# Second weight tile of the first product: its words fetched in steps 13 to 16 and its conversion begun one step later

## The chip, the cores and the metric

The kernel runs on one core of a Trainium2 chip. The metric is the device time of one execution in microseconds (us); smaller is better. The engines are named as in the profile: PE is the matrix engine (PEld its weight loads), DVE the vector engine, ACT the scalar engine, POOL the GpSimd engine, SP the engine that issues nearly all DMAs.

## The reference

Two blocks in a row. First a linear attention over 4 batches, 8 heads, 768 positions and 64 channels, worked through in blocks of 64 positions with a running state; then a mixer on the attention's output, seen as 4 x 768 x 512.

```
intra = einsum(q_b, k_b) * decay mask;  intra = einsum(intra, v_b)
inter = einsum(q_b * lam_pow, kv_state);  x = intra + inter
kv_state = lam_block * kv_state + einsum(k_b * rev_pow, v_b)
...
h = x^T @ U @ V                     (rank 32, along the 768 positions)
u = x + h^T
out = u + max(u @ w_ch1, 0) @ w_ch2 (512 -> 2048 -> 512)
```

q, k, v and lam are 32-bit floats. U, V, w_ch1 and w_ch2 arrive as 64-bit floats[...], so the kernel turns the 64-bit words into 32-bit floats itself.

## The kernel before, in words

**Stages.** The front stage (up to about 119 us of the span) does the attention and the mixer's low-rank part in 24 steps, one for each 128 positions of a batch: step s belongs to batch s // 6 and to position c = s % 6 in it. Then comes the first product u @ w_ch1 (`hidden`, L718), whose 16 weight tiles of 128 columns (`ft` = 0 to 15) meet six groups of 512 rows; its results go to HBM. Then the second product (`product`, L856) reads them back.

**One weight tile.** `w1_steps` (L232) gives the steps that make tile `ft` ready: four fetches of its 64-bit words (`fetch_part`, L129, one DMA of 128 KB each on SP), then the conversion on DVE: `one` (L153: L160), `mantissa` (L147: L149), `two` (L178), `three` (L186), `four` (L191), and the split of the 32-bit value into a high, a low and a combined part: `five` (L209), `six` (L217), `seven` (L224). Two of these hand something to ACT through `on_scalar` (L81): `one` hands over two activations that work out the exponent (L167, L168), `five` hands over a copy of the high part (L212). `three` reads what L168 wrote.

**How ACT's part is put off.** `aside(s)` (L650) runs the steps listed for step s; while it does, `on_scalar` only notes ACT's work. `on_scalar_late` (L656), in the list as `("late", s)`, then issues what was noted. From step 7 on there is one `late` in every step; it stands after `turned` and before the `aside` of the same step. So ACT's part of what `aside` does in step s is issued in step s + 1.

**One step of the front stage.** The order of all engines' work up to the first units of the first product is written out by hand (`pieces`, L561 to L583, under `manual_schedule`, L662). For s from 13 on it is: `prep(s+1)`: PE turns q and k (L355) into the PSUM banks "pq" and "pk", ACT copies them out (L358, `qt` then `kt`), and SP issues the next q and k loads; `scale(s+1)` on POOL (L383, L372); for c = 1 `fade(s)`, four activations on ACT (L392); `mix` (PE L514, DVE L517); for c = 0 `low` (PE L469, into bank "pq") and `low_rows` (DVE L489); `intra` (PE L453, then ACT's copy L458); `state` (PE L418 into bank "pk", DVE L424 or L426, SP's next v load); `turned` (ACT L550, POOL L551); `late`; `scores` (PE L400); `aside`; `inter` (PE L441); `masked` (DVE L409); `fade(s+1)` (ACT L392); `turn` (PE L531, SP's store of u L534, DVE L536 and L547). For c = 0 three pieces `next_of_low` come between (ACT L500 and L501, DVE L495, ACT L504); the result feeds the `mix` of the step after. Each of "pq" and "pk" is one bank that serves several uses in turn, so a use waits until the one before has been read out.

**Where the second tile stands.** The list at L640 to L645 says in which step each piece is run: for tile 1 the fetches in steps 8, 9, 10, 11, then `one` in 16, `mantissa` in 17, `two` in 19, `three` in 20, `four` in 21, `five` in 22, `six` in 23, and `seven` after step 23: it is `last` (L689) and runs after unit 0 of the first product (L801, L808). The first product's units 0 and 1 use tile 0, units 2 and 3 use tile 1.

Of the kernel before, what the change touches and what calls it, by code (L numbers as in the profile page):

```python
# [18 lines left out]
def kernel(  # L19
# [32 lines left out]
    NT = S // P  # L52
# [7 lines left out]
    NS = B * NT  # L60
# [18 lines left out]
    late = []  # L79
# [117 lines left out]
    def split_steps(tile_of, src, in_parts=False, scale=None, apart=False):  # L197

        st = {}

        def dst():
            if "w" not in st:
                st["w"] = wconv.tile([P, C], FP32, tag="wf", name="wf")
            return st["w"]

        def five():
            st["t"] = t = wconv.tile([P, C], FP32, tag="wt", name="wt")
            st["o"] = o = tile_of()
            nc.vector.tensor_scalar(  # L209
                t.bitcast(U32), st["w"].bitcast(U32), HI, None, ALU.bitwise_and  # L210
            )
            on_scalar(lambda: nc.scalar.copy(o[:, 0, :], t))  # L212

        def six():
            w, low = st["w"], st["o"][:, 1, :]
            st["low"] = low.bitcast(FP32) if scale is None else w
            nc.vector.tensor_tensor(  # L217
                out=low if scale is None else w, in0=w, in1=st["t"], op=ALU.subtract
            )
            if scale is not None:  # L220
                on_scalar(lambda: nc.scalar.mul(low, w, scale))

        def seven():
            nc.vector.scalar_tensor_tensor(  # L224
                st["o"][:, 2, :], st["t"], -E, st["low"], ALU.mult, ALU.add
            )

        return weight_steps(dst, src, C, in_parts=in_parts, apart=apart) + [five, six, seven]
# [3 lines left out]
    def w1_steps(ft, in_parts=False, apart=False):  # L232
        def tile_of():
            w1v[ft] = w1_pool.tile([P, 3, C], F32R, tag="w1", name="w1")
            return w1v[ft]

        cols = moe_w_ch1[:, ft * P : (ft + 1) * P].rearrange("(c p) f -> p c f", p=P)
        return split_steps(tile_of, cols, in_parts, apart=apart)
# [280 lines left out]
    uhl, ud, turned = {}, {}, {}  # L519
# [42 lines left out]
    for s in range(NS):  # L562
        b, c = divmod(s, NT)
        done = s - NT - 1
        more = s + 1 < NS
        step = [("prep", s + 1), ("scale", s + 1)] * more + [("fade", s)] * (c == 1)
        step += [("late", s - 1)] * (s == NT)
        step += [("mix", done)] * (0 <= done < NS - NT - 1)
        step += [("low", b - 1)] * (c == 0 and b > 0)
        step += [("low_rows", b - 1)] * (c == 0 and b > 0)  # L570
        step += [("intra", s)]
        step += [("next_of_low", b - 1)] * (c == 0 and b > 0)
        step += [("late", s)] * (s < NT - 1 or s == NT) + [("state", s)]
        step += [("next_of_low", b - 1)] * (c == 0 and b > 0)
        step += [("turned", done - 1)] * (done > 0) + [("late", s)] * (done >= 0)
        step += [("next_of_low", b - 1)] * (c == 0 and b > 0)
        step += [("scores", s + 1)] * more
        step += [("aside", s)] * (s >= 2 * NT)
        step += [("inter", s + 1), ("masked", s + 1)] * more
        step += [("fade", s + 1)] * (more and c > 0)  # L580
        step += [("aside", s)] * (s < 2 * NT)
        step += [("turn", done)] * (done >= 0 and done // TG < FG)
        pieces += step  # L583
# [13 lines left out]
    def v_steps():  # L597

        st = {}

        def dst():
            if "v" not in st:
                st["v"] = wconv.tile([P, C], FP32, tag="wf", name="vf")[0 : 2 * R, 0:SH]
            return st["v"]

        def parts(gs):
            for half in range(2):
                rows, cols = slice(half * R, (half + 1) * R), slice(half * SH, (half + 1) * SH)
                for g in gs:
                    yield v_hl[g * R : (g + 1) * R, cols], rows  # L610

        def five():
            st["t"] = t = wconv.tile([P, C], FP32, tag="wt", name="vt")[0 : 2 * R, 0:SH]
            nc.vector.tensor_scalar(
                t.bitcast(U32), st["v"].bitcast(U32), HI, None, ALU.bitwise_and
            )
            on_scalar(lambda: high(0))

        def high(g, copy=nc.scalar.copy):
            for out, rows in parts((g,)):  # L620
                copy(out, st["t"][rows])

        def low(g, engine):
            for out, rows in parts((g,)):
                engine.tensor_tensor(
                    out=out, in0=st["v"][rows], in1=st["t"][rows], op=ALU.subtract
                )

        halves = [moe_V[:, half * SH : (half + 1) * SH] for half in range(2)]
        return weight_steps(dst, halves, SH, 2 * R, in_parts=True) + [  # L630
            five, lambda: low(1, nc.vector), lambda: high(2, nc.vector.tensor_copy),
            lambda: low(3, nc.gpsimd),
        ]
# [5 lines left out]
    side = {}  # L639
    for steps, at in (  # L640
        (u_side, (-1, 1, 1, 2, 2)),
        (v_steps(), (0, 0, 3, 3, 4, 4, 4, 5, 4, 5)),
        (w1_steps(0, True), (3, 4, 5, 6, 8, 9, 10, 11, 13, 14, 15)),
        (w1_steps(1, True, True), (8, 9, 10, 11, 16, 17, 19, 20, 21, 22, 23, NS)),
    ):  # L645
        assert len(steps) == len(at)
        for step, n in zip(steps, at):
            side.setdefault(n, []).append(step)
# [7 lines left out]
    def on_scalar_late(s):  # L656
        for what in late:
            what()
        late.clear()
# [26 lines left out]
    run.update(aside=aside, late=on_scalar_late)  # L686
    for what, s in pieces:
        run[what](s)
    last = side.pop(NS)  # L689
    assert not side  # L690
    front_ctx.close()
# [106 lines left out]
        rest.append((unit, i, "turn", c0 + n))  # L798
    run["enter"] = enter_first_product
    head = [(pair, ft) for two in (pairs[:2], pairs[2:]) for ft in (0, 1) for pair in two]  # L800
    side = list(zip((0,), last)) + list(zip((0, 3, 3, 3, 4, 4, 4, 4), w1_steps(2)))  # L801
    for i, (pair, ft) in enumerate(head):
        before = {}
        for unit, n, *piece in rest:
# [14 lines left out]
    side = []  # L819
# [4 lines left out]
    side = w1_steps(FT - 1)  # L824
# [144 lines left out]
```

## Time and profile before

| | |
|---|---|
| median of 3 runs | 672.75 us (672.67 to 673.39) |
| the profiled execution, its own time | 673.08 us |
| its span | 671.3 us |
| PE busy | 665.1 us, 99% of the span |
| DVE, ACT, POOL busy | 74%, 41%, 17% |
| share of PE in the chain that ended last | 97% |
| steps 13 to 17: from one start of L453 to the next | 4.73 to 4.74 us |
| DMA in the stretch 40 to 104 us | mean 203 to 255 GB/s in stretches of 8 us |
| words of a weight tile, DMA of 128 KB, issue to landing | 3.0 to 4.8 us |

The timeline view gives one row for each run of like instructions: start, duration, engine, line, operation, tiles and count, and in brackets how long the engine stood idle before it and what released it. The matrix engine's rows overlap a little, since matmuls are pipelined: what matters is the start of one row against the start of the next. A wait is put down to the releaser that came last.

### The profile page before, as it was taken

To read this page: it belongs to the slowest core of one execution; us is meant where nothing else is said; L and a number is where in the kernel's file an instruction comes from. 1 tells how busy PE (TensorE), PEld (TensorE's weight loads), DVE (VectorE), ACT (ScalarE), POOL (GpSimd) and SP (SyncE) were. 2 spreads that over 40 slices of the span, in tenths; PEclk is the share of its full clock that TensorE was granted. 3 is DMA by queue.
4 is the path that set the end of the run, shared out by engine and by line. 5 is a ranking of instruction groups with operands and counts; after the bars stand their busy time and mean duration, and the time that the engine had idled before them with its cause. 6 is when DMAs were issued, how large, how long until landed. Compare 5 with 4: busy or idle time off the path is not lost.

```text
span 671.3 us, 13171 instructions
## 1 busy us (share of the span) xinstructions
PE 665.1 (99%) x5124; PEld 544.9 (81%) x5124; DVE 497.1 (74%) x873; ACT 277.3 (41%) x517; POOL 112.1 (17%) x92
## 2 busy tenths in 40 slices
PE   9999999999999999999999999999999999999997
PEld 7888989788888888888888888888888888888886
DVE  4689989877999777777797255786586775865864
ACT  4675767454555444444454121232222322322320
POOL 4465667340000000000000000030030300300300
PEclk9999999999999999999999999999999999999999
DMA  8999993254776555555577899854363363543431
GB/s 198 218 247 239 225 231 113 90 208 157 244 273 234 205 203 205 204 204 205 203 282 254 318 319 388 287 178 151 94 217 97 112 203 94 168 146 95 159 92 63
DMA packets 131775, 131.27 MB, mean 196 GB/s; under 512 B 81346, under 2 KB 89794, under 8 KB 131714
## 3 DMA queue, kind: packets, MB, share of 16 engines
q1 hardware_dynamic: 130512, 130.05, 61.2%
q8 instruction: 40, 0.66, 0.4%
q10 hardware_dynamic: 1202, 0.39, 0.2%
q14 instruction: 21, 0.17, 0.1%
HBM read 80.09 MB, written 50.33 MB: 194 GB/s over the span
## 4 chain that ended last, share of the span: by engine, by line
PE 97%; DVE 1%; DMA 1%; ACT 0%; issue 0%; ACTq 0%; DVEq 0%
PE pz L732 27%; PE pz L867 13%; PE pd L742 13%; PE pz L865 13%; PE pd L869 13%; PE px L453 4%; PE pss L400 4%; PE put L531 2%; PE pq L355 2%; PE px L441 2%; PE pk L355 1%; PE pkv L418 1%; PE pp L469 1%; PE pu L514 1%; DMA kraw<-in_k_dram 1%
## 5 line engine op out<-in xcount | busy, mean ns | idle before, releaser
L732 PE MATMUL pz<-u_hl,w 128*128 128x512 f32 x768 | 190.4, 397 | 0.0
L732 PEld LDWEIGHTS pz<-u_hl,w 128*128 128x128 f32 x768 | 144.0, 188 | 35.4 <-issue 0.4
L867 PE MATMUL pz<-w_hl,m 128*128 128x512 f32 x384 | 151.1, 396 | 0.0
L865 PE MATMUL pz<-w_hl,m 128*128 128x512 f32 x384 | 150.9, 396 | 0.0
L869 PE MATMUL pd<-w_d,m 128*128 128x512 f32 x384 | 149.5, 396 | 0.0
L848 ACT ACTIVATE m<-mt 128x512 fp32r<-128x512 f32 x96 | 60.5, 632 | 197.0 <-PE pd L869 148.9
L849 DVE SCALAR_TENSOR_TENSOR m<-rm,m 128x512 fp32r<-128x512 f32 x96 | 71.4, 746 | 53.7 <-ACT m L848 53.6
L894 POOL TENSOR_TENSOR o<-o,u 128x512 f32<-128x512 f32 x20 | 29.8, 1522 | 447.4 <-DVE o L890 447.4
L747 DVE SCALAR_TENSOR_TENSOR r<-pd,r 128x512 f32<-128x512 f32 x96 | 61.8, 686 | 53.2 <-ACT r L738 38.8
L742 PE MATMUL pd<-u_d,w 128*128 128x512 f32 x384 | 98.6, 397 | 0.0
L738 ACT ACTIVATE r<-pz 128x512 f32<-128x512 f32 x96 | 52.1, 596 | 92.7 <-PE pz L732 92.6
L867 PEld LDWEIGHTS pz<-w_hl,m 128*128 128x128 f32 x384 | 72.3, 188 | 17.7
L865 PEld LDWEIGHTS pz<-w_hl,m 128*128 128x128 f32 x384 | 72.3, 188 | 17.6
L869 PEld LDWEIGHTS pd<-w_d,m 128*128 128x128 f32 x384 | 72.3, 188 | 17.6
L742 PEld LDWEIGHTS pd<-u_d,w 128*128 128x128 f32 x384 | 72.1, 188 | 17.3
L850 DVE SCALAR_TENSOR_TENSOR m<-m 128x512 fp32r<-128x512 f32 x96 | 69.0, 721 | 0.9
L847 DVE TENSOR_SCALAR mt<-rm 128x512 uint32<-128x512 uint32 x96 | 46.1, 481 | 27.3 <-DMA rm<-r_d 26.9
L409 DVE TENSOR_TENSOR sm<-pss,mask 128x512 f32<-128x512 f32 x48 | 30.9, 685 | 7.9 <-PE pss L400 7.7
L212 ACT CAST w<-wt 128x512 fp32r<-128x512 f32 x32 | 19.9, 620 | 30.6 <-DVE wt L209 23.4
L383 POOL TENSOR_TENSOR qs<-qt,powq 128x512 f32<-128x512 f32 x20 | 26.0, 1298 | 22.0 <-ACT qt L358 19.0
L453 PEld LDWEIGHTS px<-vraw,sm 128*64 128x64 f32 x768 | 24.5, 138 | 5.2 <-issue 2.0
L400 PE MATMUL pss<-qt,kt 64*64 64x128 f32 (+1 forms) x576 | 28.1, 283 | 0.0
(88 smaller groups left out, 682.3 us busy)
## 6 DMA issues: line engine op xcount, KB each, us to landing
r_d<-r SPq DMA_DIRECT2D x96, 256.0 KB, 2.5
rm<-r_d SPq DMA_DIRECT2D x96, 256.0 KB, 2.7
words<-in_moe_w_ch_dram SPq DMA_DIRECT2D x30, 512.0 KB, 4.4
w_d<-w SPq DMA_DIRECT2D x16, 768.0 KB, 3.3
w_hl<-w_d SPq DMA_DIRECT2D x16, 512.0 KB, 6.6
vraw<-in_v_dram SPq DMA_DIRECT2D x24, 256.0 KB, 4.8
u_d<-x_nat SPq DMA_DIRECT2D x24, 256.0 KB, 3.6
u<-u_d SPq DMA_DIRECT2D x24, 256.0 KB, 3.8
```

The costliest lines, as they stand in the source:

```text
L400: nc.tensor.matmul(out=pss[rows, x, a, :], lhsT=kt[half[x], a, rows], rhs=qt[half[x], a, :], start=True, stop=True,)
L453: nc.tensor.matmul(out=px[half[t], x, a, :], lhsT=sm[:, x, a, half[t]], rhs=vr[:, 2 * a + x, :], start=(first and a == 0), stop=(a == HP - 1),
L732: nc.tensor.matmul(out=acc[g][0], lhsT=w[:, n, ct, :], rhs=uhl[g][:, n, ct, :], start=(ct == 0 and n == 0), stop=(ct == CT - 1 and n == 1),)
L738: nc.scalar.mul(rs[g], acc[g][0], 4096.0 + 1.0)
L742: nc.tensor.matmul(out=acc[g][1], lhsT=w[:, 2, ct, :], rhs=ud[g][:, ct, :], start=(ct == 0), stop=(ct == CT - 1),)
L747: nc.vector.scalar_tensor_tensor(rs[g], acc[g][1], 4096.0, rs[g], ALU.mult, ALU.add)
L848: nc.scalar.activation(out=m[:, 0], in_=t, func=AF.Relu)
L849: nc.vector.scalar_tensor_tensor(m[:, 1], r, 0.0, hi, ALU.max, ALU.subtract)
L850: nc.vector.scalar_tensor_tensor(m[:, 2], hi, E, low, ALU.mult, ALU.subtract)
L865: nc.tensor.matmul(out=pz, lhsT=m[:, 0, cols], rhs=hl[:, 0], start=first, stop=False)
L867: nc.tensor.matmul(out=pz, lhsT=m[:, 1, cols], rhs=hl[:, 1], start=False, stop=end)
L869: nc.tensor.matmul(out=pd, lhsT=m[:, 2, cols], rhs=dd, start=first, stop=end)
```

## The change

Eleven of the twelve places in the second tile's list change, and one `late` is left out. The four fetches go to steps 13 to 16, `one` to step 17, and all later pieces but `seven` one place on; `six` and `seven` both run after unit 0 of the first product. ACT's two activations (L167, L168), which `one` in step 17 hands over, would be issued by the `late` of step 18; that one is left out, so the `late` of step 19 issues them. `on_scalar_late(NS)` after the loop issues ACT's copy of the high part (L212), which `five` in step 23 hands over.

```diff
-        step += [("turned", done - 1)] * (done > 0) + [("late", s)] * (done >= 0)
+        step += [("turned", done - 1)] * (done > 0) + [("late", s)] * (done >= 0 and s != 3 * NT)
...
-        (w1_steps(1, True, True), (8, 9, 10, 11, 16, 17, 19, 20, 21, 22, 23, NS)),
+        (w1_steps(1, True, True), (13, 14, 15, 16, 17, 19, 20, 21, 22, 23, NS, NS)),
...
     for what, s in pieces:
         run[what](s)
+    on_scalar_late(NS)
     last = side.pop(NS)
...
-    side = list(zip((0,), last)) + list(zip((0, 3, 3, 3, 4, 4, 4, 4), w1_steps(2)))
+    side = list(zip((0, 0), last)) + list(zip((0, 3, 3, 3, 4, 4, 4, 4), w1_steps(2)))
```

| piece (line of its work) | step before | step after |
|---|---|---|
| four fetches (SP L140) | 8, 9, 10, 11 | 13, 14, 15, 16 |
| `one` (DVE L160) | 16 | 17 |
| ACT's L167, L168 | 17 | 19 |
| `mantissa` (DVE L149) | 17 | 19 |
| `two` (DVE L178) | 19 | 20 |
| `three` (DVE L186) | 20 | 21 |
| `four` (DVE L191) | 21 | 22 |
| `five` (DVE L209) | 22 | 23 |
| ACT's L212 | 23 | after step 23 |
| `six` (DVE L217) | 23 | after unit 0 |
| `seven` (DVE L224) | after unit 0 | after unit 0 |

No instruction is added or taken away, and the order of PE's and POOL's instructions stays as it was. Line numbers after L688 are one higher in the changed kernel, and after L801 still one higher.

## The prediction

> **What bounds the kernel now.** I read the page's engine shares and chain first, then the timelines of PE, ACT, DVE and SP around the moved pieces.
>
> ```profile
> PE 665.1 (99%) x5124; PEld 544.9 (81%) x5124; DVE 497.1 (74%) x873; ACT 277.3 (41%) x517; POOL 112.1 (17%) x92
> ...
> PE 97%; DVE 1%; DMA 1%; ACT 0%; issue 0%; ACTq 0%; DVEq 0%
> ```
>
> PE bounds every stage, so an edit that leaves PE's order alone changes the time only by the gaps it opens or closes in PE. In steps 13 to 17 the starts of L453 lie 4.73 to 4.74 us apart, every step: no gap there. The gaps of PE's timeline after 40 us are 0.16 us in step 12 (at 63.79) and 0.32 us in step 18:
>
> ```profile
> 93.35 0.60 PE L355 MATMUL pq<-ident,qraw 128*128 128x128 f32 x4
> ...
> 94.14 0.48 PE L514 MATMUL pu<-vp 128*128 128x512 f32 x1
> 94.94 1.52 PE L469 MATMUL pp<-x_nat,u_w 128*32 128x128 f32 x48 [0.32 <-ACT qt L358]
> ...
> 106.84 0.64 PE L418 MATMUL pkv<-vraw,ks 128*64 128x64 f32 x16
> ```
>
> The second row starts 0.80 us before the third, which needs bank "pq", and ACT empties it late. ACT's timeline says why, and shows the place where the same work goes:
>
> ```profile
> 92.95 0.71 ACT L167 ACTIVATE sc<-sc,vp 128x512 f32<-128x512 uint32 x1
> 93.70 0.72 ACT L168 ACTIVATE sc<-sc,vp 128x512 uint32<-128x512 f32 x1
> 94.33 0.56 ACT L358 COPY qt<-pq 128x512 f32<-128x512 f32 x1
> ...
> 103.69 1.05 ACT L392 ACTIVATE faded<-kv,powq 128x64 f32<-128x64 f32 x4
> 105.36 0.59 ACT L358 COPY qt<-pq 128x512 f32<-128x512 f32 x1 [0.62 <-PE pq L355]
> 105.84 0.59 ACT L358 COPY kt<-pk 128x512 f32<-128x512 f32 x1
> ```
>
> In step 17 the two activations stand right before the copy that frees "pq". In step 19 they will stand before the 103.69 row, where only 0.62 us of idle time is left until the next copies. The last two views are SP's and DVE's around the new place of the last fetch and of `one`:
>
> ```profile
> 87.66 0.97 SPq L279 DMA_DIRECT2D vraw<-in_v_dram  x1
> 88.73 1.71 SPq L534 DMA_DIRECT2D u_d<-x_nat  x1
> ```
>
> ```profile
> 91.85 0.42 DVE L149 TENSOR_SCALAR m<-words 128x512 uint32<-128x512 uint32 x1
> 92.99 1.29 DVE L409 TENSOR_TENSOR sm<-pss,mask 128x512 f32<-128x512 f32 x2 [0.73 <-PE pss L400]
> ...
> 96.60 1.23 DVE L489 TENSOR_SCALAR p_h<-pp 32x128 uint32<-32x128 uint32 x4 [0.40 <-PE pp L469]
> 98.06 0.42 DVE L424 COPY kv<-pkv 128x256 f32<-128x256 f32 x1 [0.23 <-PE pkv L418]
> ```
>
> The fetch of step 16 goes between the two SP rows; `one` takes the 91.85 slot. The brackets are the slack that DVE has behind it.
>
> **What the Trainium skill says.** "TensorE: Matmul & The Clock Gate", section on the array's architectural detail: ACT's and DVE's queues are strictly first in, first out. The trace agrees: qt's source was turned by 93.95, yet its copy started at 94.33, behind L168. "Perfetto Trace Analysis", section on HWDGE DMA instructions: an SP row is descriptor work after the waits, and the movement of the data is not in it; so arrival is taken from issue to landing (words: 3.0, 4.1, 4.8, 4.7, 3.4 us for the fetches of steps 6 and 8 to 11), never from the row. "SBUF — State Buffer", section on the two sides: a DVE operation with two SBUF inputs and a GpSimd one that reads SBUF shut each other out for a whole instruction. The trace agrees: L217 took 1.29 us beside POOL's L372 at 78.61, L224 1.52 us beside L544 at 131.01, against 0.68 us elsewhere.
>
> **Part 1, ACT's activations leave step 17: a gain.** In step 12, the same kind of step without them, L514 to L469 is 65.08 to 65.61, 0.53 us; in step 18 it is 0.80. Gain 0.80 - 0.53 = 0.27 us. Bounds: 0.20 (a part of the wait stays, since ACT still has copies to do), and 0.39 if L469 follows L514 as L453 does (41.16 to 41.57, 0.41 us). I take 0.27. Everything behind, ACT's chain too, moves forward with PE, so the offsets of later steps stay as they are.
>
> **Part 2, they enter step 19: a cost.** Tile 0 has the pair in the same place in step 9: L167 at 53.75, L392 at 55.12, so 1.37 us are put in. L392 goes from 103.69 to 105.06; L392 to qt is 0.95 us there (55.12 to 56.07), so qt starts at 106.01 instead of 105.36, 0.65 us late, and kt at 106.49, ending at 107.08. Queued behind: both copies, L458 and L550 of step 20. Who waits: PE's L418, which writes bank "pk" at 106.84 and needs kt's copy done. L469 started 0.05 us after its copy ended (94.89 to 94.94), so L418 starts at 107.13: a wait of 0.29 us. Step 9 had no such wait because its copies could start later without harm: there is no `fade(s)` for c = 1 and no `next_of_low` ahead. Bounds: 0.11 (the chain puts L418's work at 107.02), and 0.45 if the activations also meet late inputs of the fade. POOL's L383 starts 0.65 us late, ends near 108.0, before L441 at 108.34. I take 0.29. So part 2 takes back what part 1 gives.
>
> **Part 3, the fetches.** Out of steps 8 to 11: worth nothing, PE has no gap there and the loads land three steps (14 us) ahead of use. Into 13 to 16: each delays the store L534 behind it by some 0.9 us (L140's rows are 0.77 to 1.08), and the loads of the step after a little. The buffer that the store frees is needed by L458 two steps on: store of step 15 at 84.83, landing 3.5 us later, L458 at 91.94, so 3.6 us of slack. Covered. The last fetch is not: `one` waits for it. Issue 88.73, landing 3.0 to 4.8 us: 91.7 to 93.5, with 4.1 92.8. DVE could start at 91.85. Behind `one` are L409, L536, L547, L517, L489, L424, L495. L160 may start at 92.66 (92.99 less 0.33, its pitch) without moving L409; L489's 0.40, less the 0.27 by which PE now comes earlier, and L424's 0.23 cover 0.36 more; L504, fed by L495, ended 0.12 us ahead of L514 at 100.72. So from an arrival of about 93.1 on, PE waits in step 19, one for one. Typical landing 4.1: nothing; 4.8: 0.4 us. I take 0.10, between 0 and 0.6.
>
> **Part 4, DVE's pieces one place on.** DVE's sequence 1.25, 1.29, 0.68 us (L178, L186, L191) sits one step later with the same work around it. In step 20 the long one let L409 end at 110.44, before L453 at 110.60, and that repeats in step 21. L160 off step 16 frees 0.66 us that nobody waits for. Cost 0.
>
> **Part 5, the end.** `five` in step 23 is shorter than `six` there; L212 waits for it until about 121.6 (121.50 before), and ACT is idle until 122.99. Cost 0. After unit 0 DVE has L217 and L224, 0.63 us more (pitch of L217 at 121.18). L517 ends at 133.8, before the transposes at 134.26; ACT's L542 and L543, and behind them L738, come 0.63 us later: the second L738 ends at 136.76, and its bank is wanted by unit 2 at about 136.80. I take 0.05, from 0 to 0.2 (one operation doubled by POOL). Tile 1 is ready by 133.2, unit 2 reads it from 136.33.
>
> **Sum.** -0.27 + 0.29 + 0.10 + 0.05 = +0.17 us on the profiled execution's 673.08 (span 671.3 and 1.8 around it), so 673.25. That execution is 0.33 above the median; on the median I predict 672.75 + 0.17 = **672.9 us**.
>
> **Rivals.** (a) The gain is kept: kt's copy is in time and PE's wait in step 20 doesn't come. For it: 0.11 us separates two readings of L418's start. Against it: ACT's 1.37 us into 0.62 idle. Time: 672.75 - 0.27 = 672.5. (b) The words come moderately late, at 93.6 to 94.3: 0.5 to 1.2 us in place of the 0.10: 673.3 to 674.0, near 673.5. For it: DMA is as full in steps 13 to 16 as anywhere (225 to 237 GB/s), and 128 KB a step are added. (c) Slower: the last fetch is issued late and lands late. In step 11 SP reached its fetch 3.84 us after L453 (65.28 against 61.44), in step 16 it would be 2.73; and the longest landing in this stretch is 5.6 us (the k load of 67.12). Together: 86.00 + 3.84 + 5.6 = 95.4, PE waits 2.3 us in step 19: 675.1. It decides from an arrival of 94.4 on. Against it: steps 8 to 11 carried the same load and their fetches landed in 3.4 to 4.8. (d) That the fetches or the activations don't move as said: the instruction order of the changed kernel shows that they do, so no chance is kept for it.
>
> **Chances.** Forecast 0.62, (a) 0.17, (b) 0.16, (c) 0.05. Low end: -0.39 + 0.11 = -0.28, and the runs before reach 0.1 below their median: 672.3, rounded down. High end: -0.20 + 0.45 + 0.6 + 0.2 = +1.05: 673.8. That leaves out (c) and the end of (b). A measurement of this kernel can't tell less than 0.2% (1.35 us) from no change: faster by that would need more than all gaps that PE has in reach, 0.01; slower is (c), 0.05; the rest 0.94.
>
> **What would show it.** Right: L514 to L469 in step 18 near 0.53 us; L167 and L168 between L550 and L392 in step 19; kt's copy of step 20 ending about 0.65 us later against L355, and L418 about 0.3 us later against L453; L160 idle before it until the DMA. Wrong: L418 in its old place, L514 of step 19 waiting for L504 by more than 0.5 us, or a wait of PE on a load.

## The result and the profile after

The changed kernel takes 675.98 us (median of 7 runs, 674.39 to 676.92), before 672.75 us (7 runs, 671.55 to 673.81): ratio 1.0047, 95% interval 1.0036 to 1.0059. Run a second time it gave 1.0034 (1.0021 to 1.0047). By these two medians it is slower by 0.3% to 0.5%; 672.9 us had been forecast, with 673.8 as the upper end. Its profiled execution took 676.92 us, span 675.1, against 671.3 before.

PE's order is the same in both, so the comparison is one of starts. From L453 of step 13 to the first matmul of the first product PE took 48.56 us before (71.80 to 120.36) and 51.37 after (71.29 to 122.66): 2.81 us of the 3.8 by which the spans differ. In what follows this length is called **the stretch**. The other 1.0 us lies outside it: PE was 0.51 us ahead at step 13, and everything from the first product on took 1.50 us longer, most of it in waits that the last experiment takes up. The timeline of PE after, at steps 18 and 20:

```profile
93.63 0.47 PE L514 MATMUL pu<-vp 128*128 128x512 f32 x1
94.17 1.52 PE L469 MATMUL pp<-x_nat,u_w 128*32 128x128 f32 x48
96.41 0.34 PE L453 MATMUL px<-vraw,sm 128*64 128x64 f32 x4 [0.73 <-DVE sm L409]
97.01 1.04 PE L453 MATMUL px<-vraw,sm 128*64 128x64 f32 x28 [0.26 <-DVE sm L409]
97.87 0.64 PE L418 MATMUL pkv<-vraw,ks 128*64 128x64 f32 x16
98.44 1.10 PE L400 MATMUL pss<-qt,kt 64*64 64x128 f32 x32
100.62 0.69 PE L441 MATMUL px<-kv,qs 64*64 64x64 f32 x32 [1.07 <-DVE kv L424]
...
107.80 1.15 PE L453 MATMUL px<-vraw,sm 128*64 128x64 f32 x32
109.10 0.69 PE L418 MATMUL pkv<-vraw,ks 128*64 128x64 f32 x16
```

The first two rows show the gain: L469 follows L514 after 0.54 us (0.80 before). Then come three waits for DVE, all in step 18, and in step 20 L418 comes 1.30 us after L453 (0.98 before). DVE's timeline names the cause:

```profile
90.74 0.68 DVE L517 TENSOR_TENSOR x_nat<-pu,x_nat 128x512 f32<-128x512 f32 x1
94.35 1.41 DVE L160 TENSOR_SCALAR sc<-words 128x512 uint32<-128x512 uint32 x1 [2.93 <-DMA words<-in_moe_w_ch_dram]
95.68 1.28 DVE L409 TENSOR_TENSOR sm<-pss,mask 128x512 f32<-128x512 f32 x2
```

L160 stood 2.93 us for the words of step 16, and L409, whose result PE's L453 needs, stood behind it in DVE's queue though it needs no words. SP's timeline says when that fetch was issued:

```profile
87.41 2.58 SPq L279 DMA_DIRECT2D vraw<-in_v_dram  x1
90.05 0.78 SPq L140 DMA_DIRECT2D words<-in_moe_w_ch_dram  x1
```

L453 of step 16 started at 85.49: the fetch comes 4.56 us later, behind a v load whose row lasted 2.58 us, and the profile has 4.1 us from its issue to its landing.

### The profile page after: what moved, and what is told of

Read it like the earlier page. It is cut to its first block, busy times and chain, and to the rows that moved or that the text cites. A ratio compares the mean times of both kernels' runs of the same rounds, so it can differ in the third digit from the quotient of the medians.

```text
span 675.1 us, 13173 instructions
## 1 busy us (share of the span) xinstructions
PE 665.6 (99%) x5124; PEld 543.4 (80%) x5124; DVE 498.0 (74%) x873; ACT 277.8 (41%) x517; POOL 111.8 (17%) x92
## 4 chain that ended last, share of the span: by engine, by line
PE 91%; DMA 3%; DVE 2%; SPq 1%; ACT 1%; issue 1%; DVEq 0%; ACTq 0%
PE pz L733 27%; PE pd L743 13%; PE pz L868 13%; PE pz L866 13%; PE pd L870 13%; PE px L453 3%; PE pss L400 3%; PE put L531 2%; PE pq L355 1%; PE px L441 1%; DMA rm<-r_d 1%; PE pkv L418 1%; PE pk L355 1%; SPq L279 1%; DMA qraw<-in_q_dram 1%; PE pp L469 1%
## 5 line engine op out<-in xcount | busy, mean ns | idle before, releaser
L409 DVE TENSOR_TENSOR sm<-pss,mask 128x512 f32<-128x512 f32 x48 | 30.9, 684 | 6.1 <-PE pss L400 5.9
L212 ACT CAST w<-wt 128x512 fp32r<-128x512 f32 x32 | 19.9, 621 | 30.6 <-DVE wt L209 23.4
L453 PEld LDWEIGHTS px<-vraw,sm 128*64 128x64 f32 x768 | 24.6, 137 | 6.6 <-DVE sm L409 2.8
L383 POOL TENSOR_TENSOR qs<-qt,powq 128x512 f32<-128x512 f32 x20 | 26.0, 1299 | 22.5 <-ACT qt L358 21.8
L453 PE MATMUL px<-vraw,sm 128*64 128x64 f32 x768 | 28.2, 225 | 1.1 <-DVE sm L409 1.0
```

What stands on the lines that cost most here:

```text
L453: nc.tensor.matmul(out=px[half[t], x, a, :], lhsT=sm[:, x, a, half[t]], rhs=vr[:, 2 * a + x, :], start=(first and a == 0), stop=(a == HP - 1),
```

## The experiments

All but two start from the changed kernel. "Issue" is the time from L453 of step 16 to the last fetch.

**Fetches back in steps 8 to 11.**

```diff
-        (w1_steps(1, True, True), (13, 14, 15, 16, 17, 19, 20, 21, 22, 23, NS, NS)),
+        (w1_steps(1, True, True), (8, 9, 10, 11, 17, 19, 20, 21, 22, 23, NS, NS)),
```

> The changed kernel with its four fetches back in steps 8 to 11; all else as changed. From L453 of step 13 to the first product's first matmul PE takes 48.56 us before and 51.37 after. Theory (the last fetch arrives late, and L160 with everything behind it on DVE waits): no wait at L160, the stretch is 48.6 (0.26 gained in step 18, 0.32 lost in step 20), the time within 0.5 us of before. Rival (the pieces moved on DVE and ACT cost the time): the stretch stays above 50.5, the time about 3 us over before.

Measured: L160 doesn't wait, stretch 48.62 us, ratio 0.9998 (0.9984 to 1.0012). So the loss hangs on the fetches, as far as the timing can tell. The remaining pieces show their prices in the starts of L453: step 17 to 18 takes 5.39 us (5.65 before), step 20 to 21 takes 5.06 (4.74 before), the rest is as before.

**`one` a step later, or the fetches a step earlier.**

```diff
-        (w1_steps(1, True, True), (13, 14, 15, 16, 17, 19, 20, 21, 22, 23, NS, NS)),
+        (w1_steps(1, True, True), (13, 14, 15, 16, 18, 19, 20, 21, 22, 23, NS, NS)),
```

> The changed kernel with `one` (L160) in step 18 in place of 17; fetches stay in 13 to 16. Theory (only the wait of L160 costs): the words arrive at about 94.4, DVE reaches L160 at about 97 to 98, no wait; stretch 48.6 to 48.8, time within 0.7 us of before. Rival (the fuller DMA in steps 13 to 16 slows the loads of q, k and v, and so PE): the stretch stays above 50.

```diff
-        (w1_steps(1, True, True), (13, 14, 15, 16, 17, 19, 20, 21, 22, 23, NS, NS)),
+        (w1_steps(1, True, True), (12, 13, 14, 15, 17, 19, 20, 21, 22, 23, NS, NS)),
```

> The changed kernel with the fetches one step earlier, in 12 to 15; `one` stays in 17. Theory: the last fetch is issued at about 84.3 and lands at 88.6, ahead of DVE at 91.3; no wait, stretch 48.6. Rival (the backlog grows with the four steps wherever they lie, so that it is late by a step or more anyway): L160 waits by over 1 us, stretch above 49.5.

Measured: stretch 48.69 and 48.62 us, no wait of L160 in either, ratios 1.0004 (0.9991 to 1.0017) and 1.0000 (0.9988 to 1.0012). In the first the fetches stay in 13 to 16 and DMA is as full; q, k and v still come in time. In the second SP was behind: the last fetch was issued 5.24 us after the L453 of its own step, 15 (85.74 against 80.50), and the words were still in time. One step between the last fetch and its reader is all that was missing.

**Only the last fetch late.**

```diff
-        (w1_steps(1, True, True), (13, 14, 15, 16, 17, 19, 20, 21, 22, 23, NS, NS)),
+        (w1_steps(1, True, True), (8, 9, 10, 16, 17, 19, 20, 21, 22, 23, NS, NS)),
```

> The changed kernel with only the last of the four fetches late (steps 8, 9, 10 and 16). Theory A (backlog: four steps with 128 KB more push SP's queue behind step by step): SP reaches the fetch at about 2.7 us after L453 of step 16, as it reached the store there before; it lands at about 92 to 93 on the clock of before, L160 waits 0.5 to 1.3 us, stretch 48.6 to 49.1. Theory B (the last fetch alone is enough): issued 4 us or more after L453, L160 waits over 2 us, stretch above 50.

Measured: theory A fell. Issue 5.72 us (92.11 against 86.39), landing 4.6 us later, L160 idle for 4.62 us, stretch 52.43; ratio 1.0024 (1.0011 to 1.0037). DVE's timeline of this kernel:

```profile
91.64 0.68 DVE L517 TENSOR_TENSOR x_nat<-pu,x_nat 128x512 f32<-128x512 f32 x1
96.94 0.43 DVE L160 TENSOR_SCALAR sc<-words 128x512 uint32<-128x512 uint32 x1 [4.62 <-DMA qraw<-in_q_dram]
97.28 1.28 DVE L409 TENSOR_TENSOR sm<-pss,mask 128x512 f32<-128x512 f32 x2
```

The bracket names a q load, but L160 reads only words; 92.11 + 4.6 = 96.7 is when they landed, so this is the same wait. Four steps of added traffic are not needed for it. How far SP lags differs from one execution to the next: here SP issued the v loads 4.1 to 5.3 us after L453 in steps 12 to 16. In the profiles of before and of the changed kernel it did so after 1.65 to 1.92, at or soon after the end of L418, which frees the buffer (1.62 after L453); in the second profile of the changed kernel it was 1.66 to 3.06. The timing, 1.6 us over before and at most 2.5 by the interval, is less than the 3.9 us by which the stretch of this one execution is longer, so most executions lost less.

**The fetch ahead of the v load, and the fetch from another queue.**

```diff
-        step += [("intra", s)]
+        step += [("intra", s)] + [("aside", s + 0.5)] * (s in (13, 14, 15, 16))
...
-        (w1_steps(1, True, True), (13, 14, 15, 16, 17, 19, 20, 21, 22, 23, NS, NS)),
+        (w1_steps(1, True, True), (13.5, 14.5, 15.5, 16.5, 17, 19, 20, 21, 22, 23, NS, NS)),
```

> The changed kernel with each fetch ahead of its step's v load on SP (issued before `intra`), still in steps 13 to 16. It asks why the last fetch was issued 4.56 us after its step's L453. Theory A (it stands behind the v load, which waits for PE's L418 and then for room in the DMA queue): issued near 87.5, lands near 91.8, L160 waits under 0.7 us, stretch 48.6 to 49.2. Theory B (the queue as a whole is behind, the place in the step matters little): issued after 89, lands after 93.2, stretch above 50.

```diff
-                nc.sync.dma_start(out=out, in_=in_)
+                (last if last and i == 3 else nc.sync).dma_start(out=out, in_=in_)
...
+            dst, src, C, in_parts=in_parts, apart=apart, last=nc.scalar if apart else None
```

> The changed kernel with its last fetch, that of step 16, issued by ACT after L550 in place of SP. Theory (it is late because it stands in SP's row of issues, not because the transfer is slow): issued about 2.7 us after L453 of step 16, lands 4 us later or sooner, L160 waits under 1 us; stretch 48.6 to 49.3, the time within 0.7 us of before. Rival (the DMA engines are behind whoever issues): lands 6 us or more after its issue, L160 waits over 2 us, stretch above 50.

Measured: ahead of v, issue 0.70 us (86.04 against 85.34), landing 4.4 us later, no wait, stretch 48.61, ratio 1.0011 (0.9995 to 1.0028). From ACT's queue, issue 1.21 us (86.42 against 85.21), landing 3.7 us later, no wait, stretch 48.62, ratio 1.0001 (0.9991 to 1.0010). Both carry the changed kernel's bytes in the same steps. So the transfer wasn't slow; its place in SP's row of issues made it late. The kernel with ACT's queue shows it best, because SP was behind in that very execution: it reached the place behind its v load 5.16 us after L453. The rows of both queues (lines from 105 on are two higher there, so L536 is the store):

```profile
86.42 0.36 ACTq L140 DMA_DIRECT2D words<-in_moe_w_ch_dram  x1
...
90.37 1.00 SPq L536 DMA_DIRECT2D u_d<-x_nat  x1
```

SP's timeline of the kernel with the fetch ahead of v shows what moved there:

```profile
86.04 1.26 SPq L140 DMA_DIRECT2D words<-in_moe_w_ch_dram  x1
87.40 1.44 SPq L279 DMA_DIRECT2D vraw<-in_v_dram  x1
```

In this execution SP was in time (its v loads of steps 13 to 15 came 1.66 us after L453), so that this place is early enough when SP lags is not shown.

**Less traffic in the same steps.**

```diff
-        nc.sync.dma_start(out=u_d[s], in_=xs.pop(s))
+        x = xs.pop(s)
+        for row in () if 6 <= s <= 9 else (s, s - 4) if 10 <= s <= 13 else (s,):
+            nc.sync.dma_start(out=u_d[row], in_=x)
```

> The changed kernel with SP's stores of u (L534) left out of steps 13 to 16 and made up in 17 to 20, two a step, with the rows of the later tile in both: the residual of four tiles of 128 rows is that of other rows. DMA carries 896 KB a step in 13 to 16 in place of 1152, and SP has one issue fewer. Theory (SP reaches its v load in time and then is held, because the DMA queue has no room for more descriptors): the v load's row of step 16 shrinks from 2.6 us to about 1, the fetch is issued within 3 us of L453, lands by 92.7 on the clock of the changed kernel, L160 waits 1.3 us or less; stretch 48.6 to 49.3. Rival (what holds SP isn't the amount of data): fetch issued 4 us or more after L453, stretch above 50.5.

Measured: half of the theory held. L160's wait falls to 0.95 us and the stretch is 48.63, ratio 1.0000 (0.9986 to 1.0014). But the v load's row of step 16 still lasts 2.10 us (1.93 to 2.63 in steps 13 to 15) and the fetch is issued 3.86 us after L453; its landing takes 3.0 us. That is the shortest landing seen before, too (3.0 to 4.8), so one execution doesn't show that the lighter traffic did it. That the v row lasts long for want of room in the DMA queue is not shown either.

**ACT's part.**

```diff
-        step += [("turned", done - 1)] * (done > 0) + [("late", s)] * (done >= 0 and s != 3 * NT)
+        step += [("turned", done - 1)] * (done > 0) + [("late", s)] * (done >= 0)
```

> The changed kernel with the `late` of step 18 kept, so that L167 and L168 run in step 18, between L550 and L504. Theory: the wait of L160 stays (2 to 3 us); ACT's pair delays L504 and with it L514 of step 19 by about 1.3 us, while L418 of step 20 no longer waits (0.32 us back): stretch 52 to 52.5 by the one look, against 51.37. Rival (PE, already held by L160's wait, hides it): stretch unchanged or 0.3 shorter.

Measured: stretch 52.38, ratio 1.0041 (1.0031 to 1.0051, of before). L160's wait comes too (3.17 us), and L514 of step 19 waits 1.10 us for L504; step 20 to 21 is back at 4.73. So leaving that `late` out is worth 1.0 us to the changed kernel by the stretches (52.38 against 51.37); the timing, 1.0041 against 1.0034 for the changed kernel, is too coarse to show it.

**Two tries at the gain alone**, both from the kernel before:

```diff
-        (w1_steps(1, True, True), (8, 9, 10, 11, 16, 17, 19, 20, 21, 22, 23, NS)),
+        (w1_steps(1, True, True), (8, 9, 10, 11, 15, 17, 19, 20, 21, 22, 23, NS)),
```

> The kernel before with one edit: `one` in step 15 in place of 16, so that ACT's pair runs in step 16, where ACT is idle for 1.9 us ahead of its next copy; fetches stay in 8 to 11. Theory: the 0.27 us of step 18 is gained and nothing is lost: stretch 48.3 against 48.56 before; the time 0.3 us less, too little for the timing to tell. Rival (L160 in step 15 beside L224 makes the mask L409 late): L453 of step 16 waits, stretch 48.6 or more.

```diff
-        step += [("intra", s)]
+        step += [("late", s)] * (s == 3 * NT) + [("intra", s)]
...
-        step += [("turned", done - 1)] * (done > 0) + [("late", s)] * (done >= 0)
+        step += [("turned", done - 1)] * (done > 0) + [("late", s)] * (done >= 0 and s != 3 * NT - 1)
```

> The kernel before with one edit: the `late` of step 17 is left out and one stands in step 18 right before `intra`, so that ACT's pair L167, L168 runs where ACT is idle for 2.2 us (95.4 to 97.6 in the profile of before). Theory: step 18 gains 0.27 us and nothing is lost: stretch 48.29 against 48.56; the time 0.3 us less, which the timing can't tell from nothing. Rival (the pair makes L458 and the chain behind it up to L504 late): L514 of step 19 waits, stretch 48.6 or more.

Measured: with `one` in step 15 the stretch is 48.92, ratio 0.9996 (0.9985 to 1.0007); the rival held. L160 took 1.50 us there, beside POOL's L551, L409 came late and L453 of step 16 waited. With the pair ahead of `intra` the stretch is 48.30, as worked out. ACT's timeline of that kernel shows it in what had been idle time:

```profile
94.01 0.60 ACT L358 COPY kt<-pk 128x512 f32<-128x512 f32 x1
94.49 0.74 ACT L167 ACTIVATE sc<-sc,vp 128x512 f32<-128x512 uint32 x1
95.25 0.72 ACT L168 ACTIVATE sc<-sc,vp 128x512 uint32<-128x512 f32 x1
96.81 0.59 ACT L458 COPY x_nat<-px 128x512 f32<-128x512 f32 x1 [0.83 <-PE px L453]
```

The time of either can't be told from before's; the second is 0.9995 of it (0.9981 to 1.0009).

**The changed kernel once more.** Its profile had one more difference: at the start of the second product PE's weight loads waited 1.8 us in all for DVE, which waited for a load that landed 8.7 us after its issue.

> The changed kernel as it is, once more. It asks two things: does the last fetch land late in another execution too, and is the third part of the difference (PE's waits of 1.4 us in all at the start of the second product, L868 and L870) the change's. Theory: the wait of L160 comes again, 1.5 to 3 us long, stretch from step 13 to the first product 50 to 51.5 us; the waits of the second product's start belong to single executions of any kernel and may be missing. Rival: both come again.

Measured: stretch 51.36, L160's wait 3.09 us, issue 4.34 us; none of the waits at the second product. Its span is 2.8 us longer than before's, and the stretch is all of that. The waits at the second product came, 0.2 to 0.8 us, in three executions of other kernels and not in the rest, so they belong to single executions. The waits behind L160 are the change's. Its 22 times lie between 672.3 and 680.2 us, the lowest below before's median of 673.3, so the loss need not be the same in every execution.

## Why the prediction was wrong, by its steps

**What bounds the kernel:** right. PE's order didn't change, and the stretch changed by PE's gaps.

**Part 1, the gain in step 18:** right, 0.26 us measured for 0.27. **Part 2, the cost in step 20:** right, 0.32 for 0.29. The profile after shows ACT's rows as described:

```profile
105.14 0.63 ACT L550 ACTIVATE u_hl<-ut 128x512 fp32r<-128x512 f32 x1
105.67 0.71 ACT L167 ACTIVATE sc<-sc,vp 128x512 f32<-128x512 uint32 x1
106.42 0.72 ACT L168 ACTIVATE sc<-sc,vp 128x512 uint32<-128x512 f32 x1
107.05 1.05 ACT L392 ACTIVATE faded<-kv,powq 128x64 f32<-128x64 f32 x4
108.01 0.56 ACT L358 COPY qt<-pq 128x512 f32<-128x512 f32 x1
108.48 0.57 ACT L358 COPY kt<-pk 128x512 f32<-128x512 f32 x1
```

kt's copy ends at 109.05, L418 starts at 109.10.

**Part 3, the fetches:** the mechanism was right, the last fetch and what queues behind `one`; the step that failed is "Issue 88.73". That was one row of one execution, the store that stood in the fetch's place in step 16, 2.73 us after L453. The trace had four more of that kind; SP's timeline of before, steps 12 to 15 (the v load, then the store behind it):

```profile
68.72 2.02 SPq L279 DMA_DIRECT2D vraw<-in_v_dram  x1
70.85 0.88 SPq L534 DMA_DIRECT2D u_d<-x_nat  x1
...
73.46 2.15 SPq L279 DMA_DIRECT2D vraw<-in_v_dram  x1
75.71 0.88 SPq L534 DMA_DIRECT2D u_d<-x_nat  x1
...
78.19 2.16 SPq L279 DMA_DIRECT2D vraw<-in_v_dram  x1
80.46 0.79 SPq L534 DMA_DIRECT2D u_d<-x_nat  x1
...
82.93 1.80 SPq L279 DMA_DIRECT2D vraw<-in_v_dram  x1
84.83 0.83 SPq L534 DMA_DIRECT2D u_d<-x_nat  x1
```

With L453 at 67.06, 71.80, 76.53 and 81.27 the place behind the v load comes after 3.79, 3.91, 3.93 and 3.56 us; step 16, with a v row of 0.97 us, was the shortest of five. And this trace was an early one. Three of the experiments' kernels issue before's DMAs in before's order (fetches back in steps 8 to 11, `one` in step 15, the pair ahead of `intra`); in their profiles the store behind the v load of step 16 comes 4.73, 5.52 and 5.34 us after L453.

With 3.8 the fetch would have been put at 89.8, landing at 93.9 by the median, a loss of 0.8 us, which is rival (b); with the 4.56 that came, on the clock of before (PE was 0.51 us ahead in step 17), L160 started at 94.35 + 0.51 = 94.86. The second mis-sized term is L160 itself, taken at 0.42 us: it lasted 1.41, next to POOL's L383:

```profile
94.19 1.28 POOL L383 TENSOR_TENSOR qs<-qt,powq 128x512 f32<-128x512 f32 x1 [0.30 <-ACT qt L358]
```

It lasted 1.25 (the changed kernel again) and 1.16 (the `late` kept) beside the same L383, and 0.43 with only the last fetch late, where L383 had ended. With these two terms the prediction's formula holds: 94.86 less the 93.1 from which PE waits is 1.76, plus 0.99 of L160's length is 2.75; the two steps took 0.79 + 1.92 = 2.71 us more than the gain alone would have left (6.18 for 5.39, 6.66 for 4.74). With only the last fetch late the same sum (96.55 on the clock of before, less 93.1, plus 0.01 of length) gives 3.46 for 3.41 measured. PE met it first at L453 and L441 in step 18, though, not at L514 of step 19. So of the three signs of being wrong that the prediction named none appeared in the stretch: PE waited for DVE, and it was DVE that waited for the load.

**Part 4:** right; steps 21 to 23 take 4.74 and 3.86 us, as before. **Part 5:** 0.10 us for 0.05: from the first product's start to unit 2 it is 16.07 us (122.66 to 138.73) for 15.97.

**Rivals.** (c) is what happened, for half of the reason it gave: it worked 675.1 us out from a late issue and a late landing, and got a chance of 0.05. The late issue came, and later than it said (4.56 us for 3.84); the late landing (5.6 us) did not. That its time comes near the measured one is in part luck: the later issue and the longer L160 stand in for the landing. "Against it: steps 8 to 11 ... landed in 3.4 to 4.8" spoke of the landing, which stayed inside that (4.1); the issue was what mattered. The removed part was underrated as well: "worth nothing" was right for PE's gaps, but the four steps between the last fetch and `one` were the cover for SP's lag, and the change cut them to none. The cover was also larger than the "three steps (14 us)" given: the fetch of step 11 landed at 65.28 + 3.4 = 68.7 and L160 started at 88.08, 19.4 us later. Rival (a) leaves parts 3 and 5 out of its sum; with them it is 672.6, not 672.5.

**Left open.** What makes the v load's row last 0.97 us in one step and 2.58 in another, with the same bytes, was not found; with 256 KB a step less beside it, it still lasted 1.93 to 2.63 us in steps 13 to 16. Nor was it found what puts SP behind in one execution and not in another.

## What to carry to other kernels

A fetch that only fills a buffer early can stand anywhere in an issuing queue that runs behind; the same fetch with a reader one step on makes that queue's lag the reader's, and everything behind the reader in its engine's queue inherits it. So leave at least one step of the loop between a DMA and the first instruction that waits for it, or issue it from a queue that isn't behind. To date an issue, take the spread of all like places in the queue, over several executions, and not the row that happens to stand at the place in one of them.

## What was not expected of the hardware

The issue row of one and the same load on SP (256 KB, v) lasted from 0.37 to 2.92 us within one execution of the changed kernel, and the place behind it moved with it: 2.73 to 5.72 us after the same matmul over the executions shown.

A later arrival of the words didn't always cost more. In the changed kernel, in its second execution and with the `late` kept, L160 started 4.12, 4.28 and 4.37 us after L453 of step 17, while L383 was running on POOL, but it ended 5.53 us after it in all three, 0.3 us after L383. So PE's starts in step 18 came out the same to 0.01 us. With `one` in step 15, L160 likewise ended 0.29 us after the L551 beside it.
